# Converting the last network's weights in one stage per step, with nine stages moved into the two short slots

## Chip, cores and metric

The kernel runs on one core of a Trainium2 chip. The metric is the device time of one execution in microseconds, lower is better. The chip's engines are TensorE (PE; its weight loads are listed as PEld), VectorE (DVE), ScalarE (ACT), GpSimd (POOL) and SyncE (SP), which here issues nearly all DMAs. Each engine works through its own instructions in the order of the program and waits on semaphores for the others.

## What is computed

The reference has three parts. First an attention with 32 memory slots per head gives x with 4608 rows of 512. Then a mixture of experts sends each row to one of eight experts:

```
h = np.maximum(x[mask] @ w1[e], 0.0)
out[mask] = gate_w[mask, None] * (h @ w2[e])
```

with w1 of 512 x 1024 and w2 of 1024 x 512. Last comes one network for all rows:

```
h = x @ w_in
g = np.maximum(h, 0.0) + np.log1p(np.exp(-np.abs(h)))
return (g @ w_out).astype(np.float32)
```

with w_in of 512 x 2048 and w_out of 2048 x 512. The weights of this last network arrive as 64-bit floats, and the kernel turns them into 32-bit ones on the chip. That conversion is what the change moves.

## The kernel before

**Products.** A product in 32 bits is made of three products of split operands (`mm3`, lines 65 to 70: high times high, high times low, low times high). So every operand is split first (`split`, lines 55 to 62): one engine copies x to a high part, and another subtracts this from x and so gets the low part.

**The experts' work** (`experts`, from line 637) is cut into *units* of 512 rows of one expert (s = 0 to 7) and *slots* of 256 rows (s = 8 and s = 9, which is `LAST`); further slots, in a loop with a run-time count, come behind these when the rows need them. A unit or slot has eight steps (n = 0 to 7), one for each 128 hidden columns. The main loop (`for x in range(len(steps) + LAG)`) walks over all steps in an order that is written out by hand, and every engine's queue follows that order. In step (s, n):

- If n is 0 or 1, VectorE transposes two tiles of the next unit's rows (`turn`, line 677); after this step's first layer ScalarE and VectorE split them.
- TensorE does the first layer of (s, n): 12 matmuls into the tile ph. ScalarE (line 126) and VectorE (line 127) turn ph into the split hidden rows h.
- `part` splits 512 columns of the next expert's weights: those of w1 from two steps ago on ScalarE and VectorE, those of w2 from four steps ago on ScalarE and GpSimd. After every second one, SyncE issues the load of the weights after next.
- The conversion is advanced (below).
- TensorE does the second layer of the step two back (`LAG = 2`), into the tiles py. A unit has two py tiles, a slot one, and the pool has two buffers. So a unit's second layer, which begins in its step 2, can start once ScalarE has copied the unit before out of the first py tile.
- When that was the last step of a unit, `slot_out` has ScalarE copy py to y (line 695, four copies for a unit, two for a slot), and SyncE writes y to memory. Because of the lag this stands in step 1 of the next unit, on ScalarE's queue behind that step's part of the conversion.

In slot 8 step 3 SyncE also issues the loads of the last network's first block of rows (`block_in`), and in steps 2 to 5 of slot 9 the tiles of that block are transposed and split (`block_turn`).

**The conversion** is the generator `convert` with 32 chunks of 128 x 512 numbers. A chunk takes two *stages*, and each `next(conv, None)` runs one:

- The odd stage: one VectorE instruction finishes the chunk before (L731), whose result is split into resident tiles for the first six chunks (`first`; ScalarE, then VectorE) and written by SyncE to a scratch `wsc` for the rest. SyncE issues the load of the chunk after (L708). Then two VectorE instructions begin this chunk (L725, L726), and ScalarE takes an absolute value in place (L727), which has to wait for L726.
- The even stage: two VectorE instructions (L728, L729) and one add on GpSimd (L730).

The whole takes 65 calls: two for each chunk and one that finishes the last. The tiles d, a, b and c of the conversion are small pools; the first two hidden tiles of the last network (`begun`) use the same pools behind it, and `scratch` reads wsc back later.

Of the kernel before, what the change touches and what calls it, by code (L numbers as in the profile page):

```python
# [32 lines left out]
UNITS_E = 8  # L33
SLOTS_E = 2
LAST = UNITS_E + SLOTS_E - 1
# [14 lines left out]
def rows_in(nc, eng, dst, src, n, js=range(4)):  # L50

    return [eng.dma_start(dst[32 * j:32 * j + 32, 0:n // 32],
                          src[:, j * P:(j + 1) * P].rearrange("(a b) c -> b a c", b=32)) for j in js]
# [25 lines left out]
def full(tc, *reads):  # L79

    for w in reads:
        tc.add_to_no_dep_group("full", w.ins)


class Expert:
# [16 lines left out]
    def load(self, w, i, e, new=None, eng=None):  # L102
        (eng or self.nc.sync).dma_start(self.stage[w][i], self.dram[w][ds(e, 1), i].rearrange("o p c -> (o p) c"),
                                        **({} if new is None else dict(cond=new)))

    def part(self, w, n, lo_eng):

        i, x = n // 2, slice(n % 2 * 512, n % 2 * 512 + 512)
        split(self.nc, self.stage[w][i][:, x], self.hi[w][i][:, x], self.lo[w][i][:, x], self.nc.scalar, lo_eng)
# [541 lines left out]
def experts(tc, env):  # L651
# [5 lines left out]
    with ExitStack() as st:  # L657
# [13 lines left out]
        def gates_in(x0, T):  # L671
            ig = wk.tile([P, UNIT // P, 2], F32, name="ig", tag="ig", bufs=4)
            return ig, SP.dma_start(ig[:, 0:T // P], xs[ds(x0, T), DM:DM + 2].rearrange("(t p) c -> p t c", p=P))

        def turn(buf, k, T):
            xt = wk.tile([P, UNIT], F32, name="xt", tag="yt", bufs=2)
            V.transpose(xt[:, 0:T].rearrange("p (a b) -> p a b", b=32), raw[:, 0:T // 32, 32 * k:32 * k + 32])
            yield
            split(nc, xt[:, 0:T], hl[:, buf, 0, k, 0:T], hl[:, buf, 1, k, 0:T], A, V)
            yield  # L680
# [25 lines left out]
        def convert_in(i):  # L706
            dbl[i] = cv.tile([P, 512, 2], I32, name="d", tag="d", bufs=2)
            SP.dma_start(dbl[i].rearrange("p c w -> p (c w)"), wffn[i // 2, :, i % 2 * 512:i % 2 * 512 + 512].bitcast(I32))  # L708

        def keep(i, x, f):  # L710
            if i < len(first):
                split(nc, f, first[i][0][:, x], first[i][1][:, x], A, V)
            else:
                SP.dma_start(wsc[i, :, x], f)

        def convert():

            for i in range(2 * GC):
                d = dbl.pop(i)
                if i + 1 < 2 * GC:  # L720
                    convert_in(i + 1)
                lo, hi = d[:, :, 0], d[:, :, 1]
                a, b, c = (cv.tile([P, 512], I32, name=n, tag=n) for n in "abc")
                f, m = c.bitcast(F32), hi.bitcast(F32)
                yield (V.tensor_scalar(a, hi, 3, 0x3FFFFFF8, op0=ALU.logical_shift_left, op1=ALU.bitwise_and),  # L725
                       V.scalar_tensor_tensor(b, hi, -0x40000000, a, op0=ALU.bitwise_and, op1=ALU.bitwise_or),  # L726
                       A.activation(m, m, AF.Abs))  # L727
                yield (V.scalar_tensor_tensor(a, lo, 29, b, op0=ALU.logical_shift_right, op1=ALU.bitwise_or),  # L728
                       V.tensor_scalar(b, lo, 28, 1, op0=ALU.logical_shift_right, op1=ALU.bitwise_and),  # L729
                       G.tensor_tensor(a, a, b, ALU.add))  # L730
                V.scalar_tensor_tensor(f, m, EXP_MIN, a.bitcast(F32), op0=ALU.is_ge, op1=ALU.mult)  # L731
                keep(i // 2, slice(512 * (i % 2), 512 * (i % 2) + 512), f)

        igs, py, hs, regs = {}, {}, {}, {}
        LAG = 2
        conv = convert()
        size = lambda s: UNIT if s < UNITS_E else SLOT
        entry = lambda s: s - 1

# [7 lines left out]
        with tc.manual_schedule():  # L747
            head = lambda w, eng, hi: eng.value_load(pick[1][:, w:w + 1], min_val=0, max_val=hi)
            ea, x0 = head(0, A, E - 1), head(1, SP, E * RG - UNIT)
            for w in range(2):  # L750
                load(w, 0, ea, eng=A)
            xa = head(1, A, E * RG - UNIT)
            for x, eng, js in ((x0, SP, (0, 1)), (xa, A, (2, 3))):
                full(tc, *rows_in(nc, eng, raw, xs[ds(x, UNIT)], UNIT, js))
            e0 = head(0, SP, E - 1)
            for w in range(2):
                load(w, 1, e0)
            igs[0], w = gates_in(x0, UNIT)
            full(tc, w)
            for w in range(2):  # L760
                load(w, 2, e0)
            convert_in(0)
            for w in range(2):
                load(w, 3, e0)
            part(0, 0)
            part(0, 1)
            for k in range(4):
                list(turn(1, k, UNIT))
            expert_of(1)
            load(0, 0, *regs[1])  # L770
            rows_of(1)
            expert_of(2)
            steps = [(s, n) for s in range(LAST + 1) for n in range(FC)]
            for x in range(len(steps) + LAG):
                if x < len(steps):
                    s, n = steps[x]
                    if x == 1:
                        slot_out([py0], ig0, PAD + NT - SLOT)
                    k = n - (3 if s == 0 else 0)
                    turned = [turn(s % 2, 2 * k + i, size(s + 1)) for i in range(2)] if s < LAST and k in (0, 1) else []  # L780
                    for t in turned:
                        next(t)
                    hs[x] = layer1((s + 1) % 2, n, size(s))
                    if s == 0:
                        for w, m in ((1, n), (0, n + 2)):
                            if m < FC:
                                part(w, m)
                                if m % 2 == 1 and (w, m) != (0, 1):
                                    load(w, m // 2, *regs[1])
                    for t in turned:  # L790
                        next(t)
                    if s + 2 <= LAST and k == 2:
                        rows_of(s + 2)
                        if s > 0:
                            expert_of(s + 2)
                    for w, ago in ((0, 2), (1, 4)):
                        if x >= ago and steps[x - ago][0] < LAST:
                            after, m = steps[x - ago]
                            part(w, m)
                            if m % 2 == 1 and after + 2 <= LAST:  # L800
                                load(w, m // 2, *regs[after + 2])
                    if s == LAST - 1 and n == 3:
                        block_in(tc, env, 0)
                    if s == LAST and 2 <= n < 6:
                        block_turn(tc, env, wk, 0, n - 2, "yt", 2)
                    if s == LAST and n == 6:
                        block_ids(tc, env, 0)
                        total = nc.values_load(nslots, min_val=TABU + SLOTS_E, max_val=TAB)
                    if 0 < s < UNITS_E:
                        next(conv, None)  # L810
                        if n == 3 or (s < 3 and n == 6):
                            next(conv, None)
                if x >= LAG:
                    s, n = steps[x - LAG]
                    if n == 0:
                        py[s] = [ps_y.tile([P, 2, DM], F32, name="py", tag="y") for _ in range(size(s) // SLOT)]
                    layer2(n, py[s], hs.pop(x - LAG))
                    if n == FC - 1:
                        slot_out(py.pop(s), igs.pop(s), PAD + NT - SLOT - UNIT if s == 0 else value(2, entry(s), PAD + NT - size(s)))
            begun = []  # L820
            for n in range(2):
                ph = layer3(tc, env, ps_3, first[n], 0)
                g = cv.tile([P, 2, BLK], F32R, name="g01", tag="d", bufs=2)
                u, c, t = (cv.tile([P, BLK], F32, name=f"{x}01", tag=x) for x in "abc")
                softplus(nc, ph, u, t, c, g[:, 0], g[:, 1])
                begun.append((g[:, 0], g[:, 1]))
            ready = [layer3(tc, env, ps_3, first[2], 0)]
            halves = [scratch(env, 3 + i // 2, i % 2, i) for i in range(3)]
# [192 lines left out]
```

## Time and profile before

| | us |
|---|---|
| median of 3 runs | 1431.42 |
| lowest and highest run | 1431.37, 1433.11 |
| the profiled execution | 1429.91 |
| its span | 1428.2 |
| TensorE busy in the span | 1362.0 (95%) |
| VectorE busy | 929.5 (65%) |
| ScalarE busy | 674.8 (47%) |
| GpSimd busy | 257.5 (18%) |

The profile is of one execution. Its times count from the start of the span, and the rest of the execution's own time, 1.7 us, lies around the span. Attention and routing fill the first 165 us or so, units 0 to 7 run from 179 to 564 us, the two slots from 564 to 615 us, and the last network takes the rest. A matmul is listed with its whole way through the array (some 0.4 us), though the next one starts some 0.23 us after it. So a busy share says little about TensorE; the times between its instructions, and the idle time ahead of them, say more.

In the timeline a line gives start, duration, engine, line of the kernel, operation and tiles; in brackets stand the engine's idle time before it and what ended that.

### The profile page before, as it was taken

The numbers are of one execution on the slowest core, as the hardware profiler recorded it, in microseconds if no ns is written. First come the engines' busy times: TensorE is split into PE (matmuls) and PEld (weight loads), VectorE is DVE, ScalarE is ACT, GpSimd is POOL, SyncE is SP. The second block draws the span as 40 slices with busy tenths as digits, with TensorE's granted clock in tenths as the row PEclk, the third lists the DMA queues.
The fourth block names the chain that finished last, engine by engine and source line by source line (L and its number), as shares of the span: only waits on it lengthen the run. The fifth ranks groups of instructions, "written<-read, shape, count | busy, mean of one in ns | idle before, by whom it ended". The sixth has DMA issues, their size and how long they took to land.

```text
span 1428.2 us, 19767 instructions
## 1 busy us (share of the span) xinstructions
PE 1362.0 (95%) x7312; PEld 1095.3 (77%) x7312; DVE 929.5 (65%) x1699; ACT 674.8 (47%) x1193; POOL 257.5 (18%) x267
## 2 busy tenths in 40 slices
PE   7999599898899899999999999999999999999996
PEld 5777478676788688978888888888888888888885
DVE  4778476777877777449765656656566565665553
ACT  3556154344433443547544545445454454544543
POOL 1343234333333333400000100001000010100101
PEclk8999889989999999999999999999999999999998
DMA  9978966144244455434120200202002020000000
GB/s 357 402 296 290 332 202 147 61 118 129 85 125 132 119 174 195 119 105 133 31 59 0 59 1 8 52 0 59 1 15 45 1 59 1 19 11 0 30 1 29
DMA packets 94338, 143.03 MB, mean 100 GB/s; under 512 B 16160, under 2 KB 54048, under 8 KB 94240
## 3 DMA queue, kind: packets, MB, share of 16 engines
q1 hardware_dynamic: 86320, 120.94, 28.3%
q0 software_dynamic: 5760, 19.17, 3.6%
q10 hardware_dynamic: 2160, 1.63, 0.4%
q8 instruction: 58, 0.95, 0.3%
q14 instruction: 40, 0.33, 0.1%
HBM read 122.28 MB, written 44.62 MB: 117 GB/s over the span
## 4 chain that ended last, share of the span: by engine, by line
PE 50%; issue 6%; POOL 0%; ACT 0%; POOLq 0%; DVE 0%
PE ph L68 8%; PE po L68 8%; PE ph L70 8%; PE ph L69 8%; PE po L70 8%; PE po L69 8%; POOL out L956 0%; POOLq L1017 0%; ACT u L862 0%; ACT u L863 0%; ACT g L59 0%; DVE c L869 0%; DVE c L866 0%; POOLq L956 0%
## 5 line engine op out<-in xcount | busy, mean ns | idle before, releaser
L68 PE MATMUL ph<-hl,k 128*128 128x512 f32 (+1 forms) x536 | 204.0, 381 | 16.8 <-DMA j<-w 16.6
L69 PE MATMUL ph<-hl,k 128*128 128x512 f32 (+1 forms) x536 | 204.0, 381 | 0.0
L59 ACT ACTIVATE gh<-g 128x512 fp32r<-128x512 f32 x142 | 89.6, 631 | 236.8 <-DVE g L869 236.2
L956 POOL DMA_INDIRECT out<-ob,ids x36 | 38.8, 1076 | 779.9 <-ACT ob L955 664.3
L70 PE MATMUL ph<-hl,k 128*128 128x512 f32 (+1 forms) x456 | 173.1, 380 | 0.0
L866 DVE TENSOR_SCALAR c<-u 128x512 f32<-128x512 f32 x142 | 60.5, 426 | 169.9 <-ACT u L863 169.8
L62 DVE TENSOR_TENSOR gl<-g,gh 128x512 fp32r<-128x512 f32 x142 | 98.2, 691 | 88.0 <-ACT gh L59 88.0
L68 PE MATMUL py<-q,h 128*128 128x512 f32 x304 | 124.0, 408 | 23.9 <-ACT y L695 23.9
L862 ACT ACTIVATE u<-ph 128x512 f32<-128x512 f32 x142 | 84.8, 597 | 125.2 <-PE ph L70 125.2
L68 PEld LDWEIGHTS ph<-hl,k 128*128 128x128 f32 x536 | 101.4, 189 | 39.6 <-ACT hl L59 19.4
L70 PE MATMUL py<-q,h 128*128 128x512 f32 x304 | 122.2, 402 | 0.0
L69 PEld LDWEIGHTS ph<-hl,k 128*128 128x128 f32 x536 | 101.3, 189 | 21.3 <-DVE hl L62 1.8
L127 DVE SCALAR_TENSOR_TENSOR h<-ph,h 128x512 fp32r<-128x512 f32 (+1 forms) x88 | 54.1, 614 | 82.4 <-ACT h L126 81.9
L867 DVE TENSOR_TENSOR c<-c,u 128x512 f32<-128x512 f32 x142 | 98.2, 692 | 4.4
L869 DVE TENSOR_TENSOR g<-g,c 128x512 f32<-128x512 f32 x142 | 98.1, 691 | 4.4
L70 PEld LDWEIGHTS ph<-hl,k 128*128 128x128 f32 x456 | 85.7, 188 | 16.5 <-DVE k L62 0.2
L868 DVE SCALAR_TENSOR_TENSOR g<-ph,g 128x512 f32<-128x512 f32 x142 | 97.0, 683 | 0.3 <-ACT g L864 0.3
L863 ACT ACTIVATE u<-u 128x512 f32<-128x512 f32 x142 | 89.6, 631 | 3.9
L864 ACT ACTIVATE g<-u 128x512 f32<-128x512 f32 x142 | 89.6, 631 | 3.9
L68 PEld LDWEIGHTS py<-q,h 128*128 128x128 f32 x304 | 59.0, 194 | 38.8 <-ACT y L695 25.6
L68 PE MATMUL po<-k,gh 128*128 128x512 f32 x216 | 85.8, 397 | 0.0
L70 PE MATMUL po<-k,gl 128*128 128x512 f32 x216 | 85.6, 396 | 0.0
(251 smaller groups left out, 3077.8 us busy)
## 6 DMA issues: line engine op xcount, KB each, us to landing
k<-w SPq DMA_DIRECT2D x43, 512.0 KB
j<-w SPq DMA_DIRECT2D x43, 512.0 KB
k<-kv SPq DMA_DIRECT2D x36, 512.0 KB
d<-wffn SPq DMA_DIRECT2D x32, 512.0 KB
q<-qT SPq DMA_DIRECT2D x8, 1152.0 KB
raw<-ys SPq DMA_DIRECT2D x36, 256.0 KB
xs<-zero SPq DMA_DIRECT2D x8, 1056.0 KB
ys<-y SPq DMA_DIRECT2D x8, 1026.0 KB
```

The source lines that it names most:

```text
L59: hi_eng.activation(hi, x, AF.Copy)
L62: lo_eng.tensor_tensor(lo, x, hi.bitcast(F32), ALU.subtract)
L68: nc.tensor.matmul(out, lh, rh, start=start, stop=False)
L69: nc.tensor.matmul(out, lh, rl, start=False, stop=False)
L70: nc.tensor.matmul(out, ll, rh, start=False, stop=stop)
L862: A.activation(u, ph, AF.Abs)
L863: A.activation(u, u, AF.Exp, scale=-1.0)
L864: A.activation(g, u, AF.Ln, bias=1.0)
L866: V.tensor_scalar(c, u, 1.0, 1.0, op0=ALU.add, op1=ALU.subtract)
L867: V.tensor_tensor(c, c, u, ALU.subtract)
L868: V.scalar_tensor_tensor(g, ph, 0.0, g, op0=ALU.max, op1=ALU.add)
L869: V.tensor_tensor(g, g, c, ALU.subtract)
```

## The change

The generator itself stays. What changes is when it is advanced. Before, every step of units 1 to 7 ran one stage, and a second one in step 3 of each of them and in step 6 of units 1 and 2: 56 + 7 + 2 = 65. After, every step of units 1 to 7 runs one stage (56), and the other nine run in the slots: five in steps 0, 2, 4, 6 and 7 of slot 8, four in steps 0, 1, 6 and 7 of slot 9.

```diff
         conv = convert()
+        REST = {UNITS_E: (0, 2, 4, 6, 7), LAST: (0, 1, 6, 7)}
         size = lambda s: UNIT if s < UNITS_E else SLOT
...
-                    if 0 < s < UNITS_E:
+                    if 0 < s < UNITS_E or n in REST.get(s, ()):
                         next(conv, None)
-                        if n == 3 or (s < 3 and n == 6):
-                            next(conv, None)
```

## Rows read from the trace of the kernel before

**Rows 1.** Busy time by stretch, units 2 to 6: stretch, length, engines, clock, DMA share, GB/s

```profile
core 0: us, PE busy (x) PEld busy (x) DVE busy (x) ACT busy (x) POOL busy (x), PEclk, DMA share, GB/s
266.78:321.40 54.62, 46.24 (x193) 37.29 (x192) 40.59 (x54) 22.07 (x40) 19.26 (x15) 0.91 0.37 96
321.40:372.54 51.14, 46.32 (x194) 37.38 (x192) 39.38 (x51) 21.83 (x40) 19.45 (x15) 0.93 0.42 119
372.54:423.56 51.02, 46.50 (x194) 37.46 (x192) 39.08 (x49) 20.63 (x37) 19.45 (x15) 0.93 0.43 119
423.56:467.72 44.16, 44.16 (x194) 36.01 (x192) 34.57 (x43) 19.33 (x36) 16.82 (x13) 1.00 0.44 120
467.72:519.76 52.04, 45.89 (x194) 37.08 (x192) 40.68 (x52) 20.55 (x38) 19.97 (x15) 0.93 0.46 137
```

**Rows 2.** Who waited for whom, 220 to 640 us: total us, times, longest us

```profile
PE py L68 <- ACT y L695: 23.9, 4, 8.4
```

**Rows 3.** Timeline of ScalarE, then TensorE, at the start of unit 4

```profile
389.12 0.67 ACT L727 ACTIVATE d<-d 128x512 f32<-128x512 f32 x1 [3.56 <-DVE b L726]
389.69 2.39 ACT L695 ACTIVATE y<-py,ig 128x512 f32<-128x512 f32 x4
...
390.98 0.80 PE L68 MATMUL py<-q,h 128*128 128x512 f32 x1 [4.52 <-ACT y L695]
```

**Rows 4.** The same at the start of unit 5

```profile
432.59 0.69 ACT L727 ACTIVATE d<-d 128x512 f32<-128x512 f32 x1 [3.37 <-DVE b L726]
...
435.73 2.42 ACT L695 ACTIVATE y<-py,ig 128x512 f32<-128x512 f32 x4
...
437.32 0.39 PE L68 MATMUL py<-q,h 128*128 128x512 f32 x1
```

**Rows 5.** The stages' instructions by line: ns min/median/max, first and last start

```profile
L725 DVE TENSOR_SCALAR a<-d x32: 413/427/1516, 228.6 to 556.0; 128x512 int32<-128x512 int32 x32
L726 DVE SCALAR_TENSOR_TENSOR b<-d,a x32: 691/693/694, 230.1 to 556.4; 128x512 int32<-128x512 int32 x32
L728 DVE SCALAR_TENSOR_TENSOR a<-d,b x32: 693/1782/1794, 234.5 to 559.6; 128x512 int32<-128x512 int32 x32
L729 DVE TENSOR_SCALAR b<-d x32: 426/427/430, 236.3 to 561.4; 128x512 int32<-128x512 int32 x32
...
L731 DVE SCALAR_TENSOR_TENSOR c<-d,a x32: 677/1772/1786, 238.6 to 563.8; 128x512 f32<-128x512 f32 x32
L730 POOL TENSOR_TENSOR a<-a,b x32: 1281/1292/1306, 236.8 to 562.0; 128x512 int32<-128x512 int32 x32
```

**Rows 6.** Timeline of VectorE in unit 2: the split of a chunk that stays resident

```profile
282.82 0.69 DVE L62 TENSOR_TENSOR first<-c,first 128x512 fp32r<-128x512 f32 x1 [0.70 <-ACT first L59]
```

**Rows 7.** Timeline of VectorE, ScalarE and TensorE in slot 8, steps 1 to 3

```profile
567.83 0.76 DVE L677 STREAM_TRANSPOSE xt<-raw 128x256 f32<-128x256 f32 x2
577.30 0.42 DVE L127 SCALAR_TENSOR_TENSOR h<-ph,h 128x256 fp32r<-128x256 f32 x1 [1.59 <-ACT h L126]
...
569.83 0.39 ACT L126 ACTIVATE h<-ph 128x256 fp32r<-128x256 f32 x1 [2.12 <-PE ph L70]
...
571.77 2.41 ACT L695 ACTIVATE y<-py,ig 128x512 f32<-128x512 f32 x4
...
573.80 0.39 PE L68 MATMUL py<-q,h 128*128 128x512 f32 x1
```

**Rows 8.** Timeline of VectorE in slot 9 step 1, TensorE in slot 9 step 4

```profile
594.68 0.69 DVE L62 TENSOR_TENSOR k<-k,k 128x512 fp32r<-128x512 f32 x1
...
602.00 0.39 PE L68 MATMUL py<-q,h 128*128 128x512 f32 x1
```

**Rows 9.** Timeline of SyncE in slot 8 step 3; a wait, 220 to 640 us

```profile
581.27 2.13 SPq L52 DMA_DIRECT2D raw<-ys  x4
...
DVE a L725 <- DMA d<-wffn: 5.0, 5, 2.6
```

**Rows 10.** Busy time by stretch behind the slots (columns as in rows 1)

```profile
620.00:640.00 20.00, 17.69 (x74) 13.48 (x75) 12.38 (x22) 9.75 (x17) 0.00 (x0) 1.00 0.47 134
```

**Rows 11.** Timeline of VectorE behind the slots

```profile
618.95 0.43 DVE L866 TENSOR_SCALAR b<-a 128x512 f32<-128x512 f32 x1 [7.39 <-ACT a L863]
```

## The prediction

> **What bounds the kernel now.** I first cut the units' stretch at the first matmul of each unit's step 0 and asked for the busy time by stretch. Wherever TensorE's busy time fills a unit's window, TensorE is the bound: unit 5 takes 44.16 us with all of it busy at a granted clock of 1.00 (2.4 GHz; the lower level is 1.2), so eight steps of 5.52 us. Units 2, 3, 4 and 6 take 54.62, 51.14, 51.02 and 52.04 us, with idle time and a mean clock of 0.91 to 0.93 [rows 1]. Each window holds eight steps of TensorE work, and in its first two steps the last second layers of the unit before. Units 1 and 7 look like unit 5. So the stretch loses 10.46 + 6.98 + 6.86 + 7.88 = 32.2 us against the pace of unit 5.
>
> The list of waits then names the cause: TensorE waits four times, 23.9 us in all, for line 695, the copies of py to y [rows 2]. The other 8.3 us, 2.1 us for each stop, are what the lower clock costs around it.
>
> The timeline says why the copies are late. In unit 4, step 1, they start at 389.69, right behind L727 of the conversion, for which ScalarE sat idle 3.56 us until VectorE had done L726; TensorE starts 1.29 us after the copies' start and has lost 4.52 us [rows 3]. ScalarE is not short of time. It stands in line behind a VectorE that is behind. In unit 5 L727 comes one step earlier, the copies start at 435.73, and with the same 1.29 us py would be free at 437.02; TensorE takes it at 437.32 without idling [rows 4]. The margin is 0.3 us.
>
> **Which units stop follows from counting calls.** Odd stages carry L727. With the extra stages of before, units 2 and 3 begin on an odd stage but with an extra one in step 6 just before; units 4 and 6 begin on an even stage, so that the odd one falls into step 1, right ahead of the copies. Units 1, 5 and 7 begin on an odd stage, step 1 is even, and no extra stage lies in the three steps before. These three don't stop.
>
> **The change, part by part.** *Units.* With 8 calls in each unit every unit from 1 to 7 begins on an odd stage, step 1 is even, and nothing is doubled: all are in the state of unit 5. A step of it leaves VectorE idle time before the next one, so no debt is carried along. That gives back 32.2 us.
>
> *Unit 2 keeps a part.* The first six chunks are split into resident tiles, and call 9, at unit 2's step 0, finishes the fourth. This puts 0.70 us of waiting for ScalarE and 0.69 us of work between L731 and L725 [rows 6]: the copies come 1.39 us later, less the margin of 0.3 us, so 1.1 us of stop. It is 0 if that wait falls into idle time, and 2.5 us if call 7, in unit 1's step 6, leaves its 1.39 us as well. I take 1.1. The clock: after a stop of 2.3 us (20.00 less 17.69 in the window) it stayed 1.00 [rows 10], so nothing is added.
>
> *What moves into the slots.* Calls 57 to 65: on VectorE four L725, four L726, four L728, four L729 and five L731; on ScalarE four L727; on GpSimd four L730; on SyncE five writes to wsc and three loads of d. An odd stage costs VectorE 1.78 + 0.43 + 0.69 = 2.9 us, an even one 1.78 + 0.43 = 2.2 us [rows 5]. A slot's step takes 2.82 us of TensorE (from 573.80 to 602.00 are ten [rows 7, 8]), and VectorE idles 1.59 us in it where nothing is turned [rows 7]. So an odd stage overruns a step by 1.3 us, an even one by 0.6, and a free step behind it makes that good. The sums are not tight: what counts is where stages stand close together, or ahead of copies.
>
> *The start of slot 8.* Before, VectorE is done with step 0 at 567.83; an odd stage behind that lets L726 end at 570.75 and L727 at some 571.4. From the relu of step 1 (569.83) to the copies (571.77) ScalarE needs 1.94 us, so the copies start at 573.35 and free py at 574.65. TensorE wants it at 573.80 [rows 7]: 0.85 us of stop. Bounds: 0, if L731 takes its shortest 0.68, and 1.9, if one more instruction meets GpSimd and takes 1.1 us longer, as L728 does (0.69 or 1.78 [rows 5]).
>
> *Slot 9.* Calls 60 to 63 stand in four steps in a row: (8,6) even, (8,7) odd, (9,0) even, (9,1) odd. Ahead of the last one VectorE is 0.6 + 1.3 + 0.6 = 2.5 us behind. Before, it finished its split of (9,1) at 595.37; now that is 597.9, and L726 ends at 600.8. ScalarE then has L727 (0.6), two copies (1.2) and the relu of (9,2) (0.4), and VectorE its half of it (0.4): h is there at 603.4 to 603.6. TensorE takes h of (9,2) at 602.00 [rows 8], so it stops for some 1.5 us. Two things can be added, neither of which the trace shows in this place. GpSimd's adds (1.29 us) may hold VectorE's split behind each of the two even stages, up to 1.1 us each as for L728 [rows 5]. And in slot 8 the loads of the last network's first rows, four of 256 KB issued from 581.27 on, now stand ahead of the write of wsc and the load of d for call 61; VectorE has waited up to 2.6 us for such a d before [rows 9]. So the stop is 1.5 to 6.3 us, or 0 if the stages meet no GpSimd work (odd 1.8, even 1.1 us). I take 3.5, the middle: GpSimd works in nearly every step here, and the loads fall together with call 61. A stop of that size is nearer to the four with a clock loss than to the one without, so 2.1 us are added: 5.6 us, between 0 and 8.4.
>
> *Costed at nothing.* The pools d, a, b, c are taken over by the first hidden tiles of the last network: VectorE is idle 7.39 us before that, at 618.95 [rows 11], and the last two stages (steps 6 and 7 of slot 9) take 2.2 + 1.8 = 4.0 us of it at most; without this cover the last stage's 1.8 us would show. In SyncE's queue the new wsc writes wait for L731 with weight loads and writes of y behind them, but what those bring is used a slot later, or not by TensorE at all. GpSimd's adds delay its own splits of weights that the next slot uses, with four steps to spare.
>
> **The sum** against the profiled execution: 1429.9 - 32.2 + 1.1 + 0.85 + 5.6 = 1405.3. The median of the runs shown lies 1.5 us above that execution, so **1407 us**, with 1400 to 1412 from the bounds.
>
> **Rivals.** *All nine stages are hidden.* For it: VectorE idles over half of the slots' time there. Against: the four stages in a row. It would give 1429.9 - 32.2 + 1.5 = 1399, to 1401 with unit 2's rest. Chance 0.18.
>
> *Every stage of slot 8 and early slot 9 shows.* If VectorE and GpSimd exclude each other, each of the seven stages up to (9,1) costs its overrun and one GpSimd add of 1.29 us besides: 4 x 2.6 + 3 x 1.9 = 16.1 us, and the sum is 1416. L728's 1.78 against 0.69 us speaks for it, L726's constant 0.69 us against it [rows 5]. Chance 0.11. The Trainium skill, SBUF — State Buffer, section "Who interferes with whom", states such a rule: a VectorE instruction with two SBUF inputs and a GpSimd instruction that reads SBUF hold a shared port in turn, and the later one is blocked fully. By that rule the slots, where GpSimd's work comes twice as dense, are the worst place for these stages.
>
> *The units still stop a little.* With a margin of 0.3 us [rows 4], one more meeting with GpSimd of 1.1 us would cost 0.8 us in each of units 3 to 6, some 3 to 4 us: 1410. Against it stands that unit 5 holds the same order. Chance 0.10.
>
> *Slower.* The stops in the slots keep the granted clock at its lower level, and that slows the slots as a whole. The sixteen steps hold 45 us of matmuls; at half the clock they take 90. From 32 us of such loss on the change is lost, and at the full 45 us the time is 1444. Four stops of 4 us and more lowered the mean clock of their 51 us only to 0.91 to 0.93 [rows 1], and a slower TensorE lets VectorE catch up. Chance 0.06.
>
> **How the numbers follow.** The forecast has the remaining 0.55. A measurement here can tell about 0.2%, 3 us, from no change. All cases but the last lie far below 1428.6; I give faster 0.92, the same 0.02, slower 0.06. The range 1400 to 1417 takes in the bounds of the forecast, half of the first rival, the second and the third.
>
> **What would show it.** In the profile after, windows of a unit should all be 44.2 us (unit 2's about 45), TensorE's wait for line 695 should fall from 23.9 to 1 to 4 us, all at units 2 and 8, and a wait for h of 1 to 6 us should appear in slot 9's second layer, at the hidden tile of step 2. The forecast is wrong in its main step if units 3, 4 or 6 still stop for over 1 us, and in its second if the slots lose nothing, or more than 10 us.

## The result, and the profile after

The kernel after takes 1407.84 us (median of 4 runs, 1406.83 to 1412.61), the kernel before on the same chip 1431.39 (4 runs, 1427.68 to 1433.11). The ratio is 0.9845, with a 95% interval from 0.9816 to 0.9875: 1.5% faster. The profiled execution of after took 1406.83 us, with a span of 1404.6. Lines of the kernel after stand one or two off those of before only behind the change (L898 became L897); the lines of the conversion and of the copies have kept their numbers.

Busy time by stretch of the kernel after, cut at the first matmul of a unit's or slot's step 0, as in [rows 1]: units 2 to 6, then slots 8 and 9.

```profile
core 0: us, PE busy (x) PEld busy (x) DVE busy (x) ACT busy (x) POOL busy (x), PEclk, DMA share, GB/s
266.28:311.68 45.40, 44.43 (x194) 35.94 (x192) 37.61 (x49) 21.77 (x40) 18.40 (x14) 1.00 0.39 98
311.68:355.84 44.16, 44.16 (x194) 36.01 (x192) 34.30 (x45) 19.71 (x36) 17.32 (x14) 1.00 0.45 121
...
444.16:488.32 44.16, 44.16 (x194) 36.01 (x192) 35.31 (x45) 19.81 (x36) 17.32 (x14) 1.00 0.47 143
...
532.48:559.02 26.54, 25.64 (x158) 22.76 (x156) 22.18 (x33) 15.34 (x34) 13.00 (x11) 1.00 0.75 205
559.02:591.36 32.34, 27.58 (x158) 23.76 (x157) 23.82 (x34) 10.83 (x23) 12.84 (x11) 0.95 0.25 80
```

The same view of the two slots in the kernel before:

```profile
563.92:589.29 25.37, 25.37 (x157) 22.69 (x156) 12.70 (x25) 14.66 (x32) 10.28 (x9) 1.00 0.74 198
589.29:614.66 25.37, 25.37 (x157) 22.70 (x156) 10.53 (x20) 10.24 (x21) 7.29 (x7) 1.00 0.06 22
```

Units 3 to 6 now all take 44.16 us, with TensorE busy from end to end at 1.00; in [rows 1] only unit 5 did. Unit 2 takes 1.24 us more than that. Units 2 to 6 together went from 252.98 to 222.04 us, 30.9 us less. The slots went the other way: 25.37 to 26.54 us and 25.37 to 32.34 us, 8.1 us more. VectorE's busy time says what came into them: 12.70 became 22.18 us in slot 8, 10.53 became 23.82 in slot 9. The two sums leave 22.8 of the 23.6 us by which the span is shorter; of the other 0.8 us, 0.5 stand ahead of unit 2 and 0.3 behind the slots.

What TensorE waited for in the kernel after, 220 to 640 us (us in total, times, longest):

```profile
PE py L68 <- ACT h L126: 4.5, 2, 4.0
PE ph L68 <- issue: 2.1, 1, 2.1
PE py L68 <- ACT y L695: 1.9, 2, 1.0
...
PE py L70 <- DVE h L127: 0.2, 1, 0.2
```

The four waits for the copies, 23.9 us in [rows 2], became two of 1.9 us; waits of 4.5 and 0.2 us for the split hidden rows h are new (the line of 2.1 us is the entry of the loop behind the slots, which stops TensorE in the kernel before as well). The longest one is in slot 9. The timelines of the kernel after: VectorE, then ScalarE around that stop, then TensorE's stops from slot 8 to the loop behind the slots:

```profile
567.90 1.80 DVE L728 SCALAR_TENSOR_TENSOR a<-d,b 128x512 int32<-128x512 int32 x1
569.73 0.43 DVE L729 TENSOR_SCALAR b<-d 128x512 int32<-128x512 int32 x1
570.08 0.42 DVE L127 SCALAR_TENSOR_TENSOR h<-ph,h 128x256 fp32r<-128x256 f32 x1
570.41 1.72 DVE L62 TENSOR_TENSOR k<-k,k 128x512 fp32r<-128x512 f32 x1
572.05 1.77 DVE L731 SCALAR_TENSOR_TENSOR c<-d,a 128x512 f32<-128x512 f32 x1
573.86 0.43 DVE L725 TENSOR_SCALAR a<-d 128x512 int32<-128x512 int32 x1
574.32 0.69 DVE L726 SCALAR_TENSOR_TENSOR b<-d,a 128x512 int32<-128x512 int32 x1
577.16 0.42 DVE L127 SCALAR_TENSOR_TENSOR h<-ph,h 128x256 fp32r<-128x256 f32 x1 [2.15 <-ACT h L126]
```

```profile
575.05 0.67 ACT L727 ACTIVATE d<-d 128x512 f32<-128x512 f32 x1 [5.96 <-DVE b L726]
575.61 1.25 ACT L695 ACTIVATE y<-py,ig 128x512 f32<-128x512 f32 x2
576.75 0.38 ACT L126 ACTIVATE h<-ph 128x256 fp32r<-128x256 f32 x1
```

```profile
543.42 0.50 PE L68 MATMUL py<-q,h 128*128 128x512 f32 x1 [0.90 <-ACT y L695]
566.79 0.50 PE L68 MATMUL py<-q,h 128*128 128x512 f32 x1 [0.54 <-ACT h L126]
577.18 0.79 PE L68 MATMUL py<-q,h 128*128 128x512 f32 x1 [4.00 <-ACT h L126]
598.54 0.50 PE L68 MATMUL ph<-hl,first 128*128 128x512 f32 x1 [2.13 <-issue]
```

Read the three together. From the even stage (L728) to the end of the odd one (L726) VectorE works without a gap for seven microseconds. ScalarE has finished everything that stands ahead of L727 and then does nothing for 5.96 us, because L727 waits for L726. Behind L727, in ScalarE's order, stand two copies and the relu of step 2 (L126). TensorE needs that relu, and stops for 4.00 us. VectorE itself idles 2.15 us at the end of it, waiting for the same relu. So ScalarE is not short of time: the first layer of step 2 was through when TensorE stopped, at 573.18, and the relu could have run while ScalarE still stood, until 575.05. And no line of VectorE in the slots (530 to 595 us) waits for a d from memory.

### The profile page after: what moved, and what is told of

Read it like the earlier page. It is cut to its first block, busy times and chain, and to the rows that moved or that the text cites. A ratio compares the mean times of both kernels' runs of the same rounds, so it can differ in the third digit from the quotient of the medians.

```text
span 1404.6 us, 19784 instructions
## 1 busy us (share of the span) xinstructions
PE 1357.1 (97%) x7312; PEld 1091.5 (78%) x7312; DVE 931.3 (66%) x1699; ACT 673.7 (48%) x1193; POOL 257.0 (18%) x267
## 4 chain that ended last, share of the span: by engine, by line
PE 51%; issue 6%; POOL 0%; ACT 0%; POOLq 0%; DVE 0%
PE ph L68 8%; PE po L68 8%; PE ph L70 8%; PE ph L69 8%; PE po L70 8%; PE po L69 8%; POOL out L955 0%; POOLq L1016 0%; ACT u L861 0%; ACT u L862 0%; ACT g L59 0%; DVE c L868 0%; DVE c L865 0%; POOLq L955 0%
## 5 line engine op out<-in xcount | busy, mean ns | idle before, releaser
L59 ACT ACTIVATE gh<-g 128x512 fp32r<-128x512 f32 x142 | 89.6, 631 | 237.5 <-DVE g L868 236.9
L62 DVE TENSOR_TENSOR gl<-g,gh 128x512 fp32r<-128x512 f32 x142 | 98.2, 692 | 88.0 <-ACT gh L59 88.0
L68 PE MATMUL py<-q,h 128*128 128x512 f32 x304 | 121.3, 399 | 6.4 <-ACT h L126 4.5
L70 PE MATMUL py<-q,h 128*128 128x512 f32 x304 | 120.2, 395 | 0.2 <-DVE h L127 0.2
L126 ACT ACTIVATE h<-ph 128x512 fp32r<-128x512 f32 (+1 forms) x88 | 47.2, 537 | 100.2 <-PE ph L70 94.0
```

Source lines behind the costliest of these rows:

```text
L59: hi_eng.activation(hi, x, AF.Copy)
L62: lo_eng.tensor_tensor(lo, x, hi.bitcast(F32), ALU.subtract)
L68: nc.tensor.matmul(out, lh, rh, start=start, stop=False)
L70: nc.tensor.matmul(out, ll, rh, start=False, stop=stop)
```

## The experiments

Two questions were open. Did the units gain because of the order of the stages, as the prediction's count of calls says, or because nine calls fewer run there? And what makes the stop in slot 9: the four stages in a row, GpSimd's adds beside VectorE, or L727's place on ScalarE? The experiments e1 to e5, e7 and e9 change the kernel after, e6 and e8 the kernel before.

**e1: one call moved by two units.** Step 4 of unit 4 runs no stage, step 4 of unit 6 runs two. Unit 5 then begins on an even stage, as does unit 6, and nothing is doubled ahead of either.

```diff
-                    if 0 < s < UNITS_E or n in REST.get(s, ()):
+                    if (0 < s < UNITS_E or n in REST.get(s, ())) and (s, n) != (4, 4):
                         next(conv, None)
+                        if (s, n) == (6, 4):
+                            next(conv, None)
```

> The changed kernel, but unit 4 leaves out the stage of its step 4 and unit 6 runs two there. No unit before unit 6 runs more than one stage in a step, and the slots are as in the changed kernel. Only the order turns: units 5 and 6 now begin on an even stage, with the odd one (and its absolute value on ScalarE) in step 1, ahead of the copies of py. Theory (the place of the odd stage decides by itself): TensorE stops at the start of units 5 and 6 for line 695, 3.5 to 6.5 us each, with about 2 us of lower clock behind each, and the kernel takes 11 to 17 us more than the changed one, so 1419 to 1425. Rival (only doubled stages and the debt they leave matter): no stop at units 5 and 6, and the time stays at 1407 to 1409.

It took 1417.41 us (one run), a little below what was expected. TensorE in e1 at the starts of units 5 and 6, slot 8 and in slot 9:

```profile
417.54 0.79 PE L68 MATMUL py<-q,h 128*128 128x512 f32 x1 [2.73 <-ACT y L695]
466.20 0.50 PE L68 MATMUL py<-q,h 128*128 128x512 f32 x1 [2.72 <-ACT y L695]
551.79 0.50 PE L68 MATMUL py<-q,h 128*128 128x512 f32 x1 [0.90 <-ACT y L695]
585.55 0.80 PE L68 MATMUL py<-q,h 128*128 128x512 f32 x1 [4.00 <-ACT h L126]
```

Two stops came back, in just the two units that begin on an even stage, in a kernel whose units run as many calls as after. Order alone makes them. Their size was missed: 2.7 us instead of 3.5 and more. In the kernel before, the doubled stages ahead of units 4 and 6 may have added the rest; no run separates that. From 551.79 to 585.55 are 33.76 us; after (543.42 to 577.18) has the same 33.76, so the slots don't depend on this.

**e2: two stages back into unit 4**, those of steps 6 and 7 of slot 9, doubled in steps 3 and 6 of unit 4.

```diff
-        REST = {UNITS_E: (0, 2, 4, 6, 7), LAST: (0, 1, 6, 7)}
+        REST = {UNITS_E: (0, 2, 4, 6, 7), LAST: (0, 1)}
...
                         next(conv, None)
+                        if s == 4 and n in (3, 6):
+                            next(conv, None)
```

> The changed kernel, but two of the nine stages go back into unit 4, as second stages in its steps 3 and 6, and slot 9 has stages in steps 0 and 1 alone. Every unit still begins on an odd stage. Theory (a doubled stage in step 6 leaves VectorE behind, and the next unit's copies come late even where the order is right): one stop at the start of unit 5 for line 695, 4 to 7 us, with about 2 us of lower clock. Rival (only the order of odd and even matters): no stop at unit 5. In slot 9 the call of step 1 now only finishes the last chunk and puts no absolute value on ScalarE ahead of the copies, so the stop for the hidden tile of step 2 should fall from 4.0 to under 2 us. Together 1408 to 1413.

It took 1414.92 us (one run), 2 us over the expectation; TensorE begins the units at 180.79 us here, 3.65 us later than in after, and no edit touches what lies ahead of that. TensorE in e2, at the start of unit 5 and in the slots:

```profile
423.43 0.79 PE L68 MATMUL py<-q,h 128*128 128x512 f32 x1 [6.74 <-ACT y L695]
...
578.80 0.50 PE L68 MATMUL py<-q,h 128*128 128x512 f32 x1 [0.54 <-ACT h L126]
582.56 0.50 PE L70 MATMUL py<-q,h 128*128 128x512 f32 x1 [0.22 <-DVE h L127]
586.24 0.50 PE L70 MATMUL py<-q,h 128*128 128x512 f32 x1 [0.60 <-DVE h L127]
```

Unit 5 begins on an odd stage here and still stops, for 6.74 us: a doubled stage in step 6 leaves a debt that is not worked off by step 1. So the second cause that the prediction named, for units 2 and 3, holds by itself too. The 4.00 us in slot 9 are gone, although the four calls in a row (8,6) to (9,1) stand as before. But two calls more have run by then, so the one in (9,1) is the 65th, which only finishes the last chunk with L731 and has no L725, L726 and L727. The stop needs these, not the row alone.

**e3: the stages in the slots kept apart.** Four run in steps 4 to 7 of slot 9, where no copies of py follow until the slot is over.

```diff
-        REST = {UNITS_E: (0, 2, 4, 6, 7), LAST: (0, 1, 6, 7)}
+        REST = {UNITS_E: (0, 1, 2, 4, 6), LAST: (4, 5, 6, 7)}
```

> The changed kernel with the nine stages elsewhere in the slots: steps 0, 1, 2, 4 and 6 of slot 8 and steps 4, 5, 6 and 7 of slot 9. No four of them stand in a row before the copies in slot 9 step 1. Theory (the loss of 7 us in slot 9 is the debt of four successive stages, made visible by the absolute value ahead of the copies): the stop of 4.0 us and the lower clock vanish, under 1.5 us of stops are left in slot 9, slot 8's 0.9 us stays, and the time is 1400 to 1403. Rival (the slots have no room for nine stages wherever they stand): the stop only moves to the second half of slot 9, and the time is 1406 to 1410.

1399.97 us (4 runs, 1397.52 to 1402.38) against 1430.79 for before: ratio 0.9775, from 0.9746 to 0.9804, which lies wholly below that of after. TensorE in e3, the start of slot 8 and the first matmul behind the slots:

```profile
544.34 0.50 PE L68 MATMUL py<-q,h 128*128 128x512 f32 x1 [0.90 <-ACT y L695]
593.04 0.50 PE L68 MATMUL ph<-hl,first 128*128 128x512 f32 x1 [2.14 <-issue]
```

There is no stop in slot 9 left. Between these two lines lie 48.70 us; after needs 55.12 (543.42 to 598.54). The same nine stages cost 6.4 us less when the three steps ahead of slot 9's relu of step 2 are free of them. Slot 8's own 0.90 stays.

**e4: no GpSimd beside VectorE.** The low parts of w2 are split on VectorE, which takes most of GpSimd's work in this stretch away and gives it to VectorE.

```diff
-        part = lambda w, n: W.part(w, n, V if w == 0 else G)
+        part = lambda w, n: W.part(w, n, V)
```

> The changed kernel, but the low part of the w2 weights is subtracted on VectorE in place of GpSimd, so that GpSimd is left with the conversion's adds. VectorE gets one more instruction of 0.69 us in nearly every step of the units and slots. Theory (meeting GpSimd is what lengthens the stages from 0.69 to 1.78 us): L728 and L731 take 0.69 us nearly always, each stage costs VectorE 1.1 us less, the stop at the hidden tile of step 2 in slot 9 falls from 4.0 to 1 to 2.5 us, and the time is 1401 to 1406. Rival (the length comes from the two operands' own reads or the instruction's form): L728 and L731 stay at 1.78 us, VectorE falls further behind, units stop again, and the time is over 1415.

1401.84 us (4 runs, 1398.81 to 1405.61), ratio 0.9787 (0.9756 to 0.9818). The groups of instructions of e4 (busy us, mean ns of one, idle ahead), and TensorE and ScalarE in slot 9:

```profile
L731 DVE SCALAR_TENSOR_TENSOR c<-d,a 128x512 f32<-128x512 f32 x32 | 21.9, 685 | 2.0 <-POOL a L730 1.1 <-DMA wsc<-c 0.8
...
L728 DVE SCALAR_TENSOR_TENSOR a<-d,b 128x512 int32<-128x512 int32 x32 | 21.9, 684 | 0.0
```

```profile
574.06 0.79 PE L68 MATMUL py<-q,h 128*128 128x512 f32 x1 [3.15 <-ACT h L126]
...
571.93 0.65 ACT L727 ACTIVATE d<-d 128x512 f32<-128x512 f32 x1 [4.96 <-DVE b L726]
```

L728 fell from 1.78 us to 0.68, with nothing about it changed but what GpSimd does meanwhile. So the two do hold each other up. The Trainium skill, "SBUF — State Buffer", section "Who interferes with whom", states it: a VectorE instruction with two inputs in SBUF shares a port with GpSimd instructions that read SBUF, and the later one is blocked. The trace agrees, with 1.1 us for each meeting. From 220 to 600 us GpSimd's busy time falls from 147.7 to 46.0 us, and VectorE's falls too, from 292.1 to 266.3, although it does the splits besides. But the stop in slot 9 is still 3.15 us, above the 1 to 2.5 expected, and ScalarE still stands 4.96 us at L727. In the row of four stages VectorE now does the splits of w2 itself, and at 562.47 it waits 1.21 us for the d that L725 of call 61 reads, a wait that the kernel after does not have. At unit 2 the stop shrank from 0.97 to 0.33 us, at slot 8 it is gone. All of TensorE's waits for y and h went from 4.5 + 1.9 + 0.2 = 6.6 us to 3.15 + 0.33 = 3.5, which is 3.1 of the 8 us between the ratios. Where the rest comes from stays open; the profiled execution, 1405.61, is only 1.2 us below that of after, and begins the units 1.27 us later.

**e5: L727 one stage later.** The absolute value is issued at the front of the even stage, where L726 has long been done. Every stage stays in its step, and no instruction is added or taken out.

```diff
-                       V.scalar_tensor_tensor(b, hi, -0x40000000, a, op0=ALU.bitwise_and, op1=ALU.bitwise_or),
-                       A.activation(m, m, AF.Abs))
-                yield (V.scalar_tensor_tensor(a, lo, 29, b, op0=ALU.logical_shift_right, op1=ALU.bitwise_or),
+                       V.scalar_tensor_tensor(b, hi, -0x40000000, a, op0=ALU.bitwise_and, op1=ALU.bitwise_or))
+                yield (A.activation(m, m, AF.Abs),
+                       V.scalar_tensor_tensor(a, lo, 29, b, op0=ALU.logical_shift_right, op1=ALU.bitwise_or),
```

> The changed kernel, but the absolute value on ScalarE (L727) is issued with the even stage, one call after L726 on which it waits. No engine has less or more to do. Theory (what stops TensorE is not VectorE's debt itself, but ScalarE standing still at L727 with the relus and the copies of py queued behind it): ScalarE's wait for L726, 107.7 us in all, falls under 20 us, the stop of 4.0 us in slot 9 and those of 0.9 us at unit 2 and slot 8 shrink to under 2 us together, and the time is 1398 to 1402. Rival (VectorE's debt makes the hidden tile late whatever ScalarE does): slot 9 still stops for 2.5 us or more, and the time is 1404 to 1408.

1402.39 us (4 runs, 1400.11 to 1406.04), ratio 0.9809 (0.9783 to 0.9834). Two waits of ScalarE in the kernel after, and then those of ScalarE and TensorE in e5, 220 to 640 us:

```profile
ACT d L727 <- DVE b L726: 107.7, 32, 6.4
...
ACT h L126 <- PE ph L70: 79.2, 28, 3.9
```

```profile
ACT h L126 <- PE ph L70: 169.2, 58, 3.9
...
ACT d L727 <- DVE b L726: 3.3, 1, 3.3
...
PE py L68 <- ACT y L695: 1.5, 2, 1.0
PE py L70 <- DVE h L127: 1.2, 1, 1.2
```

In the kernel after, ScalarE had stood 107.7 us at L727; in e5 3.3 us. Its idle time has moved to the relu, which waits for TensorE (79.2, then 169.2 us): ScalarE now waits for the bound, not the bound for it. The 4.00 us in slot 9 are gone and 1.2 us are left in that slot, now for VectorE's half of h. L728 still has its median of 1.79 us (its mean fell from 1.75 to 1.68), so nearly all of GpSimd's meetings are there, and they cost little. VectorE is less late in the row of four, too: L726 of (9,1) ends 40.2 us into the slots instead of 42.5, after a wait of 1.00 us for the d of call 61 and although it met GpSimd itself and took 1.65 us. The stops come to 2.7 us where under 2 were expected, and the time just misses the expected 1398 to 1402.

**e6: the same edit in the kernel before**, with no stage moved.

> The kernel before, with all its doubled stages in the units and none in the slots; only the absolute value on ScalarE is issued with the even stage, one call after L726. Theory (the four stops of before come from ScalarE standing still at L727 ahead of the copies; how many stages a unit has matters only through that): the four stops, 23.9 us, shrink to under 4 us, and the time is 1398 to 1404, as good as the change without moving any stage. Rival (doubled stages put VectorE so far behind that the copies are late anyhow, since the splits ahead of them on ScalarE wait for VectorE's transposes): at least units 2 and 3 still stop for 3 us and more, and the time is over 1410.

1404.07 us (4 runs, 1400.26 to 1406.55), ratio 0.9826 (0.9806 to 0.9846). Waits of e6, 220 to 640 us:

```profile
ACT d L727 <- DVE b L726: 13.1, 4, 4.1
...
PE py L68 <- ACT y L695: 3.3, 1, 3.3
```

This is the root of it. Units 2, 3, 4 and 6 run nine and ten stages, doubled and out of phase as in [rows 1], and of their four stops, 23.9 us, one of 3.3 us is left, at unit 2. Unit 4, which begins at 356.48 us in e6, shows how, on ScalarE and then on VectorE:

```profile
367.59 2.41 ACT L695 ACTIVATE y<-py,ig 128x512 f32<-128x512 f32 x4
370.55 0.69 DVE L726 SCALAR_TENSOR_TENSOR b<-d,a 128x512 int32<-128x512 int32 x1
```

L726 starts 14.1 us into the unit, when TensorE already wants py (at 13.8, by [rows 1] and [rows 4]); in the kernel before it is 15.9 us. The copies don't wait for it any more and start 11.1 us into the unit instead of 17.2. So at units 3, 4 and 6 the calls that the change takes out were harmful only through L727, which held the copies behind it.

**e7: the odd stage of (9,1) one step later.**

```diff
-        REST = {UNITS_E: (0, 2, 4, 6, 7), LAST: (0, 1, 6, 7)}
+        REST = {UNITS_E: (0, 2, 4, 6, 7), LAST: (0, 2, 6, 7)}
```

> The changed kernel with one call moved: slot 9 runs its stages in steps 0, 2, 6 and 7 in place of 0, 1, 6 and 7. Theory (the odd stage of step 1 holds up the two copies and the relu of step 2 on ScalarE): the hidden tile of step 2 comes in time, and the stop passes to the tile of step 3 with 2 to 3 us in place of 4.0, since the debt of the three stages before is smaller; 1404 to 1407. Rival (the copies have no part in it): the stop stays at 3.5 us or more, on whichever tile, and the time at 1407 to 1409.

1402.69 us (one run), a little below what was expected; but this execution begins the units at 174.34 us, 2.8 us earlier than that of after, so the time says little. TensorE in e7, slot 9:

```profile
575.43 0.50 PE L68 MATMUL py<-q,h 128*128 128x512 f32 x1 [2.10 <-ACT h L126]
```

The stop goes with the stage: it now stands at the hidden tile of step 3, and is 2.10 us, as expected, instead of 4.00, since the copies no longer stand between L727 and the relu.

**e8: L727 later, two extra calls out of unit 2's way.** In the kernel before, with e5's edit, the second calls of step 6 stand in units 4 and 6 instead of 1 and 2.

```diff
-                        if n == 3 or (s < 3 and n == 6):
+                        if n == 3 or (s in (4, 6) and n == 6):
```

> The kernel before with the absolute value issued with the even stage, and the two extra stages of units 1 and 2 (step 6) moved to units 4 and 6 (step 6). All stages lie in the units. Theory (with ScalarE free, doubled stages cost TensorE nothing where no resident tile is split on the same way): the stop at unit 2 falls from 3.3 to under 1.5 us, no other unit stops for over 0.5 us, the slots keep the pace they had before, and the time is 1397 to 1402. Rival (a second stage in step 6 is late for the next unit by itself): units 5 and 7 stop for 2 us and more, and the time is 1403 to 1408.

The chip of e8 and e9 was another one, where the kernel before takes 1441.52 us (9 runs; on those of e1 to e4 and of e5 to e7 it takes 1430.79 and 1430.08), so only ratios compare. Time is lost already ahead of the units: these two begin them at 188.2 and 188.1 us, all other profiles between 173.6 and 180.8. e8: 1414.11 us, ratio 0.9817 (0.98 to 0.9835). TensorE in e8 stops once ahead of the loop, at unit 2; ScalarE just before that:

```profile
293.92 0.50 PE L68 MATMUL py<-q,h 128*128 128x512 f32 x1 [2.53 <-ACT y L695]
```

```profile
292.08 0.63 ACT L59 ACTIVATE first<-c 128x512 fp32r<-128x512 f32 x1 [2.40 <-DVE c L731]
292.62 2.40 ACT L695 ACTIVATE y<-py,ig 128x512 f32<-128x512 f32 x4
```

Units 5 and 7, behind the doubled step 6 of units 4 and 6, don't stop, where e2, with L727 in its old place, lost 6.74 us. But unit 2's stop is 2.53 us, above the 1.5 expected. That does not clear the extra call of unit 1, since without it unit 2 begins on an even stage, and the odd one of step 1 finishes a resident chunk. Its split (`first`, L59) waits 2.40 us for L731, with the copies right behind it: another waiting instruction has taken L727's place in the line.

**e9: e3 and e5 together**, on the same chip.

> The changed kernel with both single edits tried before: the absolute value issued with the even stage, and the stages in steps 0, 1, 2, 4 and 6 of slot 8 and 4 to 7 of slot 9. Theory: stops of 1.0 us at unit 2 and under 1 us at slot 8 are left and nothing in slot 9, so it gains at most 1 to 2 us on the better of the two: 1397 to 1401. Rival (the two edits take the same stop, and with the absolute value later the even stage in slot 8 step 1 now holds up the copies): 1401 to 1405.

1413.4 us, ratio 0.9809 (0.9795 to 0.9823). Waits of e9, 220 to 640 us:

```profile
PE py L68 <- ACT y L695: 2.0, 2, 1.0
```

Slot 9 doesn't stop, and no gain over either edit alone is shown: both take the same stop. The intervals of e3, e4, e5, e6, e8 and e9 overlap, but for those of e3 and e6, which lie 0.0002 apart; none of the six is shown to be the best. All have a smaller ratio than after; only for e3 do the intervals lie apart.

## Why the prediction was right, and where it was not

The time was 1407.84 us against 1407, within the range. The steps:

- *The units give back 32.2 us, and unit 2 keeps 1.1*: 31.1 us were forecast, 30.9 measured. Units 3 to 6 take unit 5's 44.16 us. Unit 2's stop is 0.97 us, and its window is 1.24 longer. The count of calls was the right tool: e1 and e2 show each of its two clauses alone, an even stage at a unit's start and a doubled one in step 6.
- *Slot 8 loses 0.85 us*: TensorE stops for 0.90 us at the copies; the window is 1.17 longer. Here as in unit 2 a stop costs 0.27 us more than its idle time.
- *Slot 9: a stop of 3.5 us and 2.1 for the clock*: it is one stop of 4.00 us at the very tile that was named, two small ones of 0.54 and 0.2 us, and a granted clock of 0.95 over the window, which stands for 0.05 x 32.34 = 1.6 us of TensorE's time. The window is 6.97 us longer, not 5.6; the 0.6 us that are left are no more than three stops at 0.27 us. Of the two causes that could lengthen the stop, one was real and one zero. GpSimd's meetings held VectorE's splits behind the even stages (L62 took 1.72 us instead of 0.69); no wait for a d came up, but it does in e4 and e5, where VectorE reaches call 61 earlier. The choice of the middle was half right in reason, and its size came out partly by luck. The prediction has L726 of (9,1) end 36.9 us into the slots and TensorE want the hidden tile at 38.1. It ended at 42.5, and TensorE, after its earlier stops, wanted the tile at 40.7: two errors, of 5.6 and 2.6 us, of which the second hides part of the first. The two meetings make 2.1 of the 5.6 us. Another 1.0 is VectorE's own wait for the relu of (9,0), which stood behind the L727 before on ScalarE, a wait that the prediction did not count.
- *Costed at nothing*: the pools and SyncE's queue. No wait in the slots of after points to either. The sum over units and slots leaves 0.8 us, and as a gain, not a loss.
- *The rivals*. "All hidden", 1399 to 1401, is what e3 makes of the same nine stages, at 1399.97: that rival failed through the placement of four of them, not through their work. "Every stage shows", 1416, fell: VectorE and GpSimd do block each other (in e5 even L726, the argument against it, takes some 1.65 us twice), but only the debt in front of (9,1) reached TensorE with more than 1 us. GpSimd's work is not twice as dense in the slots either: 10.28 and 7.29 of 25.37 us before, against 16.82 of 44.16 in unit 5 [rows 1]. "The units still stop" fell with four windows of 44.16. "Slower" fell: the clock was 0.95 in one slot and 1.00 in the other.
- *What the prediction did not see*: it read [rows 3] rightly, "ScalarE stands in line", but took the lateness of VectorE as the thing to cure, as the change does. e5 and e6 show that the line itself is the cause. With L727 issued a stage later VectorE is still late (1.8 us less than before in e6's unit 4, 2.3 less than after in e5's slot 9), and TensorE hardly notices. In slot 9 the two effects are not separated.
- *The clock*: that a short stop leaves it at 1.00 was taken from one stretch, [rows 10]. It did not bear on the sum, since unit 2 and slot 8 did stay at 1.00, but it does not hold in general (last section). The 2.3 us of idle time there are two waits, of 2.14 and 0.18 us.
- *The bounds*: the terms as given add up to 1399 at the lower end, not 1400.

What stays partly open is unit 2. It stops in after and in every experiment, for 0.3 to 3.3 us. The prediction put it down to the wait and work of the resident split [rows 6], 1.39 us. In after, units 2 and 3 hold the same order but for this split, and the copies start 13.59 us into unit 2 and 12.18 into unit 3, so 1.41 later. That fits, but no run took the split away.

## What to carry to other kernels

An instruction that waits for another engine stops all that stands behind it on its own queue, so ask of every long wait not what it costs its engine but who needs the next instructions in line. Issue it a stage later, when its operand has long been there: here that changed no engine's work and removed most of TensorE's stops in both kernels. Then look at what stands in line next, as e8 shows. And where background work is spread over steps, its phase matters as much as its amount: look at which part of it falls just ahead of the copies that free an accumulator.

## What was not expected of the hardware

TensorE stops for 2.1 us behind the slots, at the entry of a loop, in every one of these kernels. In the profiles of before and after the granted clock stayed at 1.00 there; in all nine experiments it fell. After, then e3, ten microseconds around that stop:

```profile
596.00:606.00 10.00, 7.40 (x30) 4.99 (x29) 6.46 (x12) 5.17 (x9) 0.00 (x0) 1.00 0.33 84
```

```profile
590.60:600.60 10.00, 7.86 (x27) 5.58 (x26) 5.24 (x9) 4.41 (x8) 0.00 (x0) 0.83 0.36 86
```

The stop is 2.13 us in the one and 2.14 in the other. A mean of 0.83 over 10 us, between the levels of 1.2 and 2.4 GHz, cost 0.17 x 10 = 1.7 us of TensorE's full pace. It can go both ways within one execution. These are e1's two stops at line 695, of 2.73 and 2.72 us:

```profile
414.00:427.00 13.00, 10.27 (x38) 7.99 (x37) 6.40 (x10) 6.12 (x11) 3.52 (x4) 0.87 0.83 210
463.00:476.00 13.00, 10.28 (x46) 8.08 (x45) 7.91 (x11) 6.12 (x11) 4.20 (x4) 1.00 0.73 200
```

The first cost 0.13 x 13 = 1.7 us of clock, the second none. What decides between the two isn't shown by these runs; a stop of two to three microseconds is best costed with a clock loss between zero and these 1.7 us.
